# Two tokens per partition for the q and k transposes, reordered first loads, and a first FFN tile that begins on two units

## The chip, the cores and the metric

The kernel runs on one core of a Trainium2 chip. The metric is the device time of one execution in microseconds, lower is better. The numbers of the profile come from one profiled execution.

## The reference

Sliding-window causal attention (batch 8, 8 heads, 576 tokens, head size 64, window 64) feeds a gated FFN. All inputs and the output are float32.

```python
scores = scale * np.matmul(q, k.transpose(0, 1, 3, 2))
mask = (rel >= 0) & (rel < window)            # rel = query position - key position, window = 64
scores = np.where(mask, scores, -1000000000.0)
attn = np.exp(scores - max) / sum
attn_out = np.matmul(attn, v)                 # (8, 8, 576, 64)
x = attn_out.transpose(0, 2, 1, 3).reshape(4608, 512)
gate = np.maximum(x @ w_gate, 0.0)            # w_gate, w_val: 512 x 1536
val = x @ w_val
out = gate * val @ w_out                      # w_out: 1536 x 512, out: 4608 x 512
```

## The kernel before

**Attention units.** The 4608 tokens are cut into 24 units of 192 tokens, three per batch; a unit holds all eight heads. For each unit `u_load` brings q, k and v in, with four DMAs for q and four for k (two heads each, 32 partitions) and two for v. In q and k a partition holds six neighbouring tokens of a head, so 1536 bytes in a row. `u_cast` makes float16 copies on GpSimd (q of the first three units on ScalarE). `u_trans` transposes q and k in 32x32 blocks on VectorE, four instructions per unit, so that the head's elements lie on the partitions. Each writes with the step that the load's layout gives:

```python
nc.vector.transpose(dst.rearrange("p h (i j) -> p h j i", i=32),
                    src.rearrange("p (h j) e -> p h j e", h=2))
```

Here `i` runs over 32 partitions and `j` over the six tokens of each, so neighbouring results go six float16 elements (12 bytes) apart. `u_st` multiplies keys by queries on TensorE, `u_exp` takes the exponentials on ScalarE, `u_mask` zeroes on VectorE what lies outside the window, `u_pv` multiplies by v and sums the weights on TensorE, `u_copy` brings that to SBUF on ScalarE. `u_sum` (a transpose and a reciprocal), `u_back` (a transpose back) and `u_norm` (a product that writes the FFN's input `xt`) run on VectorE.

**FFN tiles.** `ffn(t)` works on one tile of tokens: 512 first, then ten of 384, and 256 last. For each of 12 slices of the hidden size it does two groups of four matmuls (`wg`, `wv`), a relu on ScalarE (`relu`) and a product on VectorE (`gate`, into `g_sb`). Then, for each 128 tokens, 12 matmuls with `wo` (`op`), a copy on ScalarE and a DMA out (`evac`). The hidden slices use four PSUM buffers (`f_ps`), attention four others (`a_ps`).

**The order.** All instructions are put in order when the program is built. `Weaver` keeps a planned clock that the FFN's matmuls (and a unit's scores and pv) advance, and a heap of pieces of attention work with planned times. Before each matmul group `advance` issues what is due. `plan_unit(u, T)` lays a unit's pieces around its time T: transposes from T - 6.8 (the first three units T - 2), scores at T, pv at T + 4.4, sums at T + 7.6, back at T + 8.9, norm at T + 9.9; loads at T - 22. Units 0 to 4 have times written by hand, later ones come every 13.2 planned us from 64. Ahead of a tile, `while normed[0] * U < starts[t] + sizes[t]: W.pop()` issues pieces early until all the tile's tokens are normed. Within an engine, instructions run in the order in which they were issued.

**The weights.** Nine chunks of 1 MB (three each of gate, value and out) go through three stage buffers (`w_load`); `w_cast` makes them float16, one half on GpSimd and one on ScalarE. All nine and the units' loads are issued on SyncE's queue (SP); only the q of unit 0 is issued on ScalarE's.

Of the kernel before, what the change touches and what calls it, by code (L numbers as in the profile page):

```python
# [9 lines left out]
FP32 = mybir.dt.float32  # L10
FP16 = mybir.dt.float16
# [31 lines left out]
def kernel(  # L43
# [19 lines left out]
    NF = DF // 128  # L63
    G = 4
    scale = 1.0 / float(D) ** 0.5
    sizes = [512] + [384] * 10 + [256]
    starts = [sum(sizes[:i]) for i in range(len(sizes))]
    assert sum(sizes) == NT

# [51 lines left out]
    def w_load(wt, src, j):  # L121
        stg = stage.tile([128, 4, 512], FP32, name="stg")
        if wt is wo:
            nc.sync.dma_start(stg, src.rearrange("(c p) n -> p c n", p=128)[:, 4 * j:4 * j + 4])
        else:
            nc.sync.dma_start(stg, src.rearrange("(c p) n -> p c n", p=128)[:, :, 512 * j:512 * j + 512])
        return stg

    def w_cast(wt, j, stg, half):
        cs = slice(2 * half, 2 * half + 2)  # L130
        dst = wo[:, 4 * j + 2 * half:4 * j + 2 * half + 2] if wt is wo else wt[:, cs, 512 * j:512 * j + 512]
        if half == 0:
            nc.gpsimd.tensor_copy(dst, stg[:, cs])
        else:
            nc.scalar.copy(dst, stg[:, cs])

    def u_load(u):
        b, uu = divmod(u, UB)  # L140
        d = units[u] = {}
        for name, src in (("k", k), ("q", q)):
            nat = d[name] = a_in.tile([128, 2, 384], FP32, name=name + "n")
            for g in range(G):
                eng = nc.scalar if (u == 0 and name == "q") else nc.sync
                eng.dma_start(
                    nat[32 * g:32 * g + 32],
                    src[b, 2 * g:2 * g + 2, U * uu:U * uu + U].rearrange(
                        "h (i j) d -> i h (j d)", i=32))
        vn = d["v"] = a_in.tile([128, 2, H, 64], FP32, name="vn")  # L150
        for w in range(2):
            k0 = U * uu - 64 + 128 * w
            p0 = max(0, -k0)
            nc.sync.dma_start(vn[p0:128, w], v[b, :, k0 + p0:k0 + 128].rearrange("h p d -> p h d"))

    def u_cast(u, name):
        d = units[u]
        if name == "v":
            v16 = d["v16"] = a_16.tile([128, 2, H, 64], FP16, name="v16")
            if u % UB == 0:  # L160
                nc.gpsimd.memset(v16[0:64, 0], 0.0)
                nc.gpsimd.tensor_copy(v16[64:128, 0], d["v"][64:128, 0])
                nc.gpsimd.tensor_copy(v16[:, 1], d["v"][:, 1])
            else:
                nc.gpsimd.tensor_copy(v16, d["v"])  # L165
        else:
            c16 = d[name + "16"] = a_16.tile([128, 768], FP16, name=name + "16")
            src = d[name].rearrange("p h e -> p (h e)")
            if name == "q" and u < UB:
                nc.scalar.copy(c16, src)  # L170
            else:
                nc.gpsimd.tensor_copy(c16, src)  # L172

    def u_trans(u, name, dh):
        d = units[u]
        src = d[name + "16"].rearrange("p (b e) -> p b e", e=64)[:, :, 32 * dh:32 * dh + 32]
        if name == "q":
            if dh == 0:
                d["qT"] = a_16.tile([128, 2, 2, U], FP16, name="qT")
            dst = d["qT"][:, dh]  # L180
        else:
            c0 = 64 + U * (u % UB)
            dst = kTs[(u // UB) % 2][:, dh, :, c0:c0 + U]
        nc.vector.transpose(dst.rearrange("p h (i j) -> p h j i", i=32),  # L184
                            src.rearrange("p (h j) e -> p h j e", h=2))

    def u_st(u):
        d = units[u]
# [23 lines left out]

    def u_mask(u, g):
        p = units[u]["p"][g]
        nc.vector.tensor_tensor(  # L215
            p, p, mask.rearrange("p w c -> p (w c)")[:, None, :].to_broadcast([128, 2, 256]), MUL)

    def u_pv(u):
# [46 lines left out]
        normed[0] = u + 1  # L265

    def plan_unit(u, T):
        fast = u < UB
        if not fast:
            W.at(T - 22, lambda: u_load(u))  # L270
        s = 0.5 if fast else 1.7
        for i, (name, dh) in enumerate((("k", 0), ("k", 1), ("q", 0), ("q", 1))):
            W.at(T - s * (4 - i), lambda name=name, dh=dh: u_trans(u, name, dh))
        for i, name in enumerate(("k", "q", "v")):
            W.at(T - s * 4 - (1.0 if fast else 4 - i), lambda name=name: u_cast(u, name))
        W.at(T, lambda: u_st(u))
        for g in range(G):
            W.at(T + 0.8 + 0.6 * g, lambda g=g: u_exp(u, g))
            W.at(T + 1.5 + 0.6 * g, lambda g=g: u_mask(u, g))
        W.at(T + 4.4, lambda: u_pv(u))  # L280
        for g in range(G):
            W.at(T + 5.2 + 0.5 * g, lambda g=g: u_copy(u, g))
        W.at(T + 7.6, lambda: u_sum(u))
        W.at(T + 8.9, lambda: u_back(u))
        W.at(T + 9.9, lambda: u_norm(u))


    def ffn(t):
        n = sizes[t]
        xt = xts[t]  # L290
        g_sb = g_sb_p.tile([128, NF, 512], FP16, name="g_sb")
        dt = 4 * n / 2400.0
        done = set()

        def relu(r_sb, h1):
            nc.scalar.activation(r_sb[:, 0:n], h1[:, 0:n], ACT.Relu)  # L296

        def gate(f, r_sb, h2):
            nc.vector.tensor_tensor(g_sb[:, f, 0:n], r_sb[:, 0:n], h2[:, 0:n], MUL)  # L299
            done.add(f)  # L300

        for f in range(NF):
            fs = bass.ds(f * 128, 128)
            hs = []
            for i, wt in enumerate((wg, wv)):
                W.advance(W.clock)
                h = f_ps.tile([128, 512], FP32, name=f"h{i}", tag="h")
                for c in range(NC):
                    nc.tensor.matmul(h[:, 0:n], wt[:, c, fs], xt[:, c, 0:n],  # L309
                                     start=(c == 0), stop=(c == NC - 1))  # L310
                hs.append(h)
                W.clock += dt
                if i == 0:
                    r_sb = f_sb.tile([128, 512], FP32, name="r_sb")
                    W.at(W.clock, lambda r_sb=r_sb, h=h: relu(r_sb, h))
                else:
                    W.at(W.clock, lambda f=f, r_sb=r_sb, h=h: gate(f, r_sb, h))

        def evac(sub, op):
            o_sb = f_sb.tile([128, DM], FP32, name="o_sb")  # L320
            nc.scalar.copy(o_sb, op)  # L321
            nc.sync.dma_start(out[bass.ds(starts[t] + sub * 128, 128)], o_sb)

        for sub in range(n // 128):
            op = f_ps.tile([128, DM], FP32, name="op", tag="h")
            ss = bass.ds(sub * 128, 128)
            for f0 in range(0, NF, 4):
                W.advance(W.clock)
                for f in range(f0, f0 + 4):
                    while f not in done:  # L330
                        W.pop()
                    nc.tensor.matmul(op, g_sb[:, f, ss], wo[:, f],  # L332
                                     start=(f == 0), stop=(f == NF - 1))
                W.clock += 4 * 512 / 2400.0
            W.at(W.clock, lambda sub=sub, op=op: evac(sub, op))

    with tc.manual_schedule():
        for u in range(UB):
            u_load(u)
        constants()  # L340
        at = 21.0
        for half in range(3):
            for wt, src in ((wg, moe_w_gate), (wv, moe_w_val)):
                def go(wt=wt, src=src, j=half, at=at):
                    stg = w_load(wt, src, j)
                    for hf in range(2):
                        W.at(at, lambda hf=hf: w_cast(wt, j, stg, hf))
                W.at(at - 12.0, go)
                at += 2.8
        for j in range(3):  # L350
            def go(j=j, at=at):
                stg = w_load(wo, moe_w_out, j)
                for hf in range(2):
                    W.at(at, lambda hf=hf: w_cast(wo, j, stg, hf))
            W.at(at - 12.0, go)
            at += 2.8
        for u, T in enumerate((10.0, 15.3, 20.6, 46.0, 52.0)):
            plan_unit(u, T)
        for u in range(5, NU):
            plan_unit(u, 64.0 + 13.2 * (u - 5))  # L360
        W.advance(27.0)
        for t in range(len(sizes)):
            while normed[0] * U < starts[t] + sizes[t]:
                W.pop()
            ffn(t)
        W.drain()

# [29 lines left out]
```

## Time and profile before

| | us |
|---|---|
| runs shown (three) | 416.14, 416.37, 418.63; median 416.37 |
| the profiled execution | 418.46 |
| its span, first to last instruction | 416.7 |
| TensorE busy / VectorE / ScalarE / GpSimd | 348.0 / 310.5 / 188.3 / 79.7 |
| mean granted TensorE clock | 0.97 |

In lines of the profile, L184 is line 184 of the kernel. A group's row names line, engine, operation, output and input, shape and count, then busy time in us and the mean of one in ns, then the idle time of the engine just before these instructions and what ended it. A timeline row begins with the start and the length in us. A wait's row reads: who waited for whom, us in total, times, the longest.

### The profile page before, as it was taken

The numbers are of one execution on the slowest core, as the hardware profiler recorded it, in microseconds if no ns is written. First come the engines' busy times: TensorE is split into PE (matmuls) and PEld (weight loads), VectorE is DVE, ScalarE is ACT, GpSimd is POOL, SyncE is SP. The second block draws the span as 40 slices with busy tenths as digits, with TensorE's granted clock in tenths as the row PEclk, the third lists the DMA queues.
The fourth block names the chain that finished last, engine by engine and source line by source line (L and its number), as shares of the span: only waits on it lengthen the run. The fifth ranks groups of instructions, "written<-read, shape, count | busy, mean of one in ns | idle before, by whom it ended". The sixth has DMA issues, their size and how long they took to land.

```text
span 416.7 us, 8098 instructions
## 1 busy us (share of the span) xinstructions
PE 348.0 (84%) x3120; PEld 193.6 (46%) x3120; DVE 310.5 (75%) x448; ACT 188.3 (45%) x385; POOL 79.7 (19%) x103
## 2 busy tenths in 40 slices
PE   0333696969798898798899799899899899799996
PEld 0222242435444545455555445445446546446583
DVE  3877556895958978968987978977987988786231
ACT  2355272725344445355446336346436545445241
POOL 3330343232111211121213101211203202000000
PEclk9999999887989999999999999999999999899999
DMA  8972998378005507306516307307417324020011
GB/s 183 238 271 87 298 282 220 89 229 213 2 25 161 131 30 201 89 26 182 123 51 183 86 35 195 89 27 198 105 52 197 71 94 111 0 77 2 25 53 50
DMA packets 71159, 49.82 MB, mean 120 GB/s; under 512 B 49616, under 2 KB 61904, under 8 KB 71120
## 3 DMA queue, kind: packets, MB, share of 16 engines
q1 hardware_dynamic: 70800, 48.91, 43.0%
q8 instruction: 24, 0.39, 0.4%
q10 hardware_dynamic: 320, 0.39, 0.4%
q14 instruction: 15, 0.12, 0.1%
HBM read 39.85 MB, written 9.44 MB: 118 GB/s over the span
## 4 chain that ended last, share of the span: by engine, by line
PE 50%; DVE 32%; ACT 6%; issue 5%; DMA 5%; SPq 1%; POOL 0%; DVEq 0%; ACTq 0%; POOLq 0%
PE h L309 31%; PE op L332 12%; DVE qT L184 10%; DVE kT L184 6%; DVE sT L244 4%; PE pv L226 4%; DVE rs L252 4%; PE st L199 4%; DVE g_sb L299 3%; DVE xt L261 3%; ACT xs L239 3%; DMA kn<-in_k_dram 3%; DMA stg<-in_moe_w_out_dram 2%; ACT p L211 1%; DVE rT L246 1%
## 5 line engine op out<-in xcount | busy, mean ns | idle before, releaser
L309 PE MATMUL h<-xt,wg 128*128 128x384 f16 (+2 forms) x576 | 123.2, 338 | 18.4 <-DVE xt L261 12.0
L309 PE MATMUL h<-xt,wv 128*128 128x384 f16 (+2 forms) x576 | 122.7, 337 | 1.2 <-DVE g_sb L299 1.2
L299 DVE TENSOR_TENSOR g_sb<-r_sb,h 128x384 f16<-128x384 f32 (+2 forms) x144 | 80.0, 562 | 57.3 <-PE h L309 42.8
L296 ACT ACTIVATE r_sb<-h 128x384 f32<-128x384 f32 (+2 forms) x144 | 71.1, 494 | 97.6 <-PE h L309 86.0
L332 PE MATMUL op<-wo,g_sb 128*128 128x512 f16 x432 | 99.9, 387 | 4.2 <-ACT r_sb L296 4.2
L309 PEld LDWEIGHTS <-wg 128*128 128x128 f16 x576 | 56.6, 100 | 61.7 <-issue 27.5
L309 PEld LDWEIGHTS <-wv 128*128 128x128 f16 x576 | 56.9, 101 | 41.8 <-issue 7.6
L184 DVE STREAM_TRANSPOSE kT<-k 128x384 f16<-128x384 f16 x48 | 69.0, 1456 | 6.1 <-POOL k L172 6.1
L211 ACT ACTIVATE p<-st 128x512 f16<-128x512 f32 x96 | 52.6, 608 | 38.5 <-PE st L199 38.0
L184 DVE STREAM_TRANSPOSE qT<-q 128x384 f16<-128x384 f16 x48 | 68.9, 1448 | 0.0
L332 PEld LDWEIGHTS <-g_sb 128*128 128x128 f16 x432 | 41.9, 100 | 54.9 <-ACT r_sb L296 4.7
L215 DVE TENSOR_TENSOR p<-p,mask 128x512 f16<-128x512 f16 x96 | 41.3, 451 | 20.5 <-ACT p L211 19.7
L321 ACT COPY o_sb<-op 128x512 f32<-128x512 f32 x36 | 21.1, 586 | 60.9 <-PE op L332 58.8
L199 PE MATMUL st<-qT,kT 32*128 32x128 f16 x768 | 20.0, 228 | 34.1 <-DVE qT L184 33.9
L239 ACT COPY xs<-pv 128x384 f32<-128x384 f32 x96 | 40.0, 498 | 14.3 <-PE pv L226 14.3
L172 POOL CAST k<-kn 128x768 f16<-128x768 f32 x24 | 20.7, 861 | 114.0 <-DMA kn<-in_k_dram 69.2
L199 PEld LDWEIGHTS <-kT 32*128 32x128 f16 x768 | 13.1, 97 | 44.0 <-issue 31.6
L244 DVE STREAM_TRANSPOSE sT<-xs 128x768 f32<-128x768 f32 x24 | 23.6, 982 | 12.1 <-ACT xs L239 12.1
L226 PE MATMUL pv<-p,v 128*64 128x128 f16 x384 | 25.7, 232 | 7.2 <-DVE p L215 7.2
L165 POOL CAST v<-vn 128x1024 f16<-128x1024 f32 x16 | 16.6, 1040 | 60.8 <-PE pv L226 35.7
L261 DVE TENSOR_TENSOR xt<-xs,rs 128x768 f16<-128x768 f32 (+2 forms) x35 | 26.9, 794 | 0.1
L172 POOL CAST q<-qn 128x768 f16<-128x768 f32 x21 | 17.4, 827 | 48.4 <-DVE qT L184 35.8
(27 smaller groups left out, 133.3 us busy)
## 6 DMA issues: line engine op xcount, KB each, us to landing
vn<-in_v_dram SPq DMA_DIRECT2D x40, 256.0 KB, 3.9
kn<-in_k_dram SPq DMA_DIRECT2D x96, 96.0 KB, 3.5
out_dram<-o_sb SPq DMA_DIRECT2D x36, 256.0 KB, 2.0
qn<-in_q_dram SPq DMA_DIRECT2D x92, 96.0 KB, 2.9
stg<-in_moe_w_gate_dram SPq DMA_DIRECT2D x3, 1024.0 KB, 6.7
stg<-in_moe_w_val_dram SPq DMA_DIRECT2D x3, 1024.0 KB, 7.2
stg<-in_moe_w_out_dram SPq DMA_DIRECT2D x3, 1024.0 KB, 7.3
vn<-in_v_dram SPq DMA_DIRECT2D x8, 128.0 KB, 2.9
```

Of the source, the lines that this page charges most:

```text
L184: nc.vector.transpose(dst.rearrange("p h (i j) -> p h j i", i=32), src.rearrange("p (h j) e -> p h j e", h=2))
L199: nc.tensor.matmul(d["st"][g][:, (2 * hh + w) * 128:(2 * hh + w + 1) * 128], kT[rows, dh, hh, ks + 128 * w:ks + 128 * w + 128], d["qT"][ro ...
L211: nc.scalar.activation(d["p"][g].rearrange("p h c -> p (h c)"), d["st"][g], ACT.Exp, scale=scale)
L215: nc.vector.tensor_tensor(p, p, mask.rearrange("p w c -> p (w c)")[:, None, :].to_broadcast([128, 2, 256]), MUL)
L226: nc.tensor.matmul(pv[64 * e:64 * e + 64, s, 64 * w:64 * w + 128], d["v16"][:, w, 2 * g + e] if s == 0 else (ones0 if u % UB == 0 and w == ...
L239: nc.scalar.copy(d["xs"][:, g], d["pv"][g])
L244: nc.vector.transpose(sT.rearrange("p g b c -> p g (b c)"), d["xs"][:, :, 1])
L261: nc.vector.tensor_tensor(xt_tile(t)[:, :, a - t0:z - t0], d["xs"][:, :, 0, a - lo:z - lo], rs[:, :, a - lo:z - lo], MUL)
L296: nc.scalar.activation(r_sb[:, 0:n], h1[:, 0:n], ACT.Relu)
L299: nc.vector.tensor_tensor(g_sb[:, f, 0:n], r_sb[:, 0:n], h2[:, 0:n], MUL)
L309: nc.tensor.matmul(h[:, 0:n], wt[:, c, fs], xt[:, c, 0:n], start=(c == 0), stop=(c == NC - 1))
L332: nc.tensor.matmul(op, g_sb[:, f, ss], wo[:, f], start=(f == 0), stop=(f == NF - 1))
```

## The change

- **Layout.** The 192 tokens of a unit are taken as three blocks of 64, and a partition holds two neighbouring tokens of each block. A load's runs are 512 bytes, and the transposes write in steps of two elements (4 bytes). Loads of q and k are now one DMA per head, 16 per unit instead of eight; units 1 and 2 share one set (`qk_load(1, 2)`).
- **First loads.** For the first three units the second head of each pair is issued on ScalarE's queue. The order is q,k of unit 0, its v, q,k of units 1 and 2, their v. A small exponential is issued between them.
- **Engines.** q of unit 0 is cast on VectorE, other q on GpSimd. Both halves of each weight chunk are cast on GpSimd. Three masks of units 0 and 1 run on GpSimd.
- **Order.** Tile sizes become 512, 256, then ten of 384. Tile 0 begins its first two hidden slices with the 384 tokens of units 0 and 1 and does the other 128 tokens once unit 2 is normed. Planned times of loads, casts and units change; units from 5 on start at max(T4 + 8, 69).

```diff
-    sizes = [512] + [384] * 10 + [256]
+    sizes = [512, 256] + [384] * 10
...
-        if half == 0:
-            nc.gpsimd.tensor_copy(dst, stg[:, cs])
-        else:
-            nc.scalar.copy(dst, stg[:, cs])
+        nc.gpsimd.tensor_copy(dst, stg[:, cs])
...
+    def qk_load(u, n):
+        b, uu = divmod(u, UB)
         for name, src in (("k", k), ("q", q)):
+            nat = a_in.tile([128, 2, 3 * n, 128], FP32, name=name + "n", tag=f"{name}n{n}", bufs=3 - n)
             for g in range(G):
+                for h in range(2):
+                    eng = nc.scalar if u < UB and h == 1 else nc.sync
+                    eng.dma_start(
+                        nat[32 * g:32 * g + 32, h],
+                        src[b, 2 * g + h, U * uu:U * uu + U * n].rearrange(
+                            "(m i j) d -> i m (j d)", i=32, j=2))
...
-            if name == "q" and u < UB:
-                nc.scalar.copy(c16, src)
+            if name == "q" and u == 0:
+                nc.vector.tensor_copy(c16, src)
...
-        nc.vector.transpose(dst.rearrange("p h (i j) -> p h j i", i=32),
-                            src.rearrange("p (h j) e -> p h j e", h=2))
+        nc.vector.transpose(dst.rearrange("p h (m i j) -> p h m j i", i=32, j=2), src)
...
-        nc.vector.tensor_tensor(
+        eng = nc.gpsimd if (u == 0 and g > 1) or (u == 1 and g > 2) else nc.vector
+        eng.tensor_tensor(
...
+        if u > 4:
+            W.at(T - 22, lambda: qk_load(u, 1))
+            W.at(T - 22, lambda: v_load(u))
         for i, (name, dh) in enumerate((("k", 0), ("k", 1), ("q", 0), ("q", 1))):
-            W.at(T - s * (4 - i), lambda name=name, dh=dh: u_trans(u, name, dh))
+            W.at(T - (0.5 if u < 5 else 1.7) * (4 - i), lambda name=name, dh=dh: u_trans(u, name, dh))
         for i, name in enumerate(("k", "q", "v")):
-            W.at(T - s * 4 - (1.0 if fast else 4 - i), lambda name=name: u_cast(u, name))
+            W.at(T - (3.0 if u < 5 else 11 - i), lambda name=name: u_cast(u, name))
...
+        early = {}
+        if t == 0:
+            while normed[0] < 2:
+                W.pop()
+            for f in range(2):
+                for i, wt in enumerate((wg, wv)):
+                    early[f, i] = f_ps.tile([128, 512], FP32, name=f"h{i}", tag="h")
+                    hidden(early[f, i], wt, f, 0, 2 * U)
+        ready(t)
...
+                if (f, i) in early:
+                    h = early[f, i]
+                    hidden(h, wt, f, 2 * U, n)
...
+        qk_load(0, 1)
+        warm = consts.tile([128, 2], FP32)
+        nc.vector.memset(warm, 0.0)
+        nc.scalar.activation(warm[:, 1:2], warm[:, 0:1], ACT.Exp)
+        v_load(0)
+        qk_load(1, 2)
+        v_load(1)
+        v_load(2)
         constants()
...
+        t_load, t_land = 8.0, 19.5
+        for c in chunks[:6]:
+            W.at(t_load, lambda c=c, at=t_land: chunk(*c, at))
+            t_load, t_land = t_load + 2.7, t_land + 2.7
+        W.at(t_load, lambda: qk_load(3, 1))
+        W.at(t_load, lambda: v_load(3))
+        t_load, t_land = t_load + 6.0, t_land + 6.0
+        T3 = t_land + 4.0
+        for c in chunks[6:]:
+            W.at(t_load, lambda c=c, at=t_land: chunk(*c, at))
+            t_load, t_land = t_load + 2.7, t_land + 2.7
+        W.at(t_load, lambda: qk_load(4, 1))
+        W.at(t_load, lambda: v_load(4))
+        T4 = t_land + 7.0
+        for u, T in enumerate((7.2, 14.0, 19.0, T3, T4)):
             plan_unit(u, T)
         for u in range(5, NU):
-            plan_unit(u, 64.0 + 13.2 * (u - 5))
-        W.advance(27.0)
+            plan_unit(u, max(T4 + 8.0, 69.0) + 13.2 * (u - 5))
+        W.advance(26.0)
```

Here `chunk` loads one weight chunk and plans its two casts at `at`, and `hidden` is one group of four matmuls over the columns that it is given.

More of the change, by code (lines that the diff above doesn't have):

```diff
@@ L131, in w_cast, with v_load @@
         dst = wo[:, 4 * j + 2 * half:4 * j + 2 * half + 2] if wt is wo else wt[:, cs, 512 * j:512 * j + 512]
-        if half == 0:
-            nc.gpsimd.tensor_copy(dst, stg[:, cs])
-        else:
-            nc.scalar.copy(dst, stg[:, cs])
-    def u_load(u):
+        nc.gpsimd.tensor_copy(dst, stg[:, cs])
+    def qk_load(u, n):
         b, uu = divmod(u, UB)
-        d = units[u] = {}
         for name, src in (("k", k), ("q", q)):
-            nat = d[name] = a_in.tile([128, 2, 384], FP32, name=name + "n")
+            nat = a_in.tile([128, 2, 3 * n, 128], FP32, name=name + "n", tag=f"{name}n{n}", bufs=3 - n)
             for g in range(G):
[L145 to L150, printed above, removed]
+                for h in range(2):
[4 more added lines that the diff above has]
+                            "(m i j) d -> i m (j d)", i=32, j=2))
+            for i in range(n):
+                units.setdefault(u + i, {})[name] = nat[:, :, 3 * i:3 * i + 3]
+    def v_load(u):
+        b, uu = divmod(u, UB)
+        d = units[u]
+        vn = d["v"] = a_in.tile([128, 2, H, 64], FP32, name="vn", bufs=2)
         for w in range(2):
@@ L166, in u_cast @@
         else:
-            c16 = d[name + "16"] = a_16.tile([128, 768], FP16, name=name + "16")
-            src = d[name].rearrange("p h e -> p (h e)")
-            if name == "q" and u < UB:
-                nc.scalar.copy(c16, src)
+            c16 = d[name + "16"] = a_16.tile([128, 2, 3, 128], FP16, name=name + "16")
+            src = d[name]
+            if name == "q" and u == 0:
+                nc.vector.tensor_copy(c16, src)
             else:
@@ L175, in u_trans @@
         d = units[u]
-        src = d[name + "16"].rearrange("p (b e) -> p b e", e=64)[:, :, 32 * dh:32 * dh + 32]
+        src = d[name + "16"].rearrange("p h m (j e) -> p h m j e", j=2)[:, :, :, :, 32 * dh:32 * dh + 32]
         if name == "q":
@@ L267, in plan_unit @@
     def plan_unit(u, T):
[L268 to L271, printed above, removed]
+        if u > 4:
+            W.at(T - 22, lambda: qk_load(u, 1))
+            W.at(T - 22, lambda: v_load(u))
         for i, (name, dh) in enumerate((("k", 0), ("k", 1), ("q", 0), ("q", 1))):
-            W.at(T - s * (4 - i), lambda name=name, dh=dh: u_trans(u, name, dh))
+            W.at(T - (0.5 if u < 5 else 1.7) * (4 - i), lambda name=name, dh=dh: u_trans(u, name, dh))
         for i, name in enumerate(("k", "q", "v")):
-            W.at(T - s * 4 - (1.0 if fast else 4 - i), lambda name=name: u_cast(u, name))
+            W.at(T - (3.0 if u < 5 else 11 - i), lambda name=name: u_cast(u, name))
         W.at(T, lambda: u_st(u))
@@ L285, in plan_unit, with ready @@
         W.at(T + 9.9, lambda: u_norm(u))
+    def ready(t):
+        while normed[0] * U < starts[t] + sizes[t]:
+            W.pop()
     def ffn(t):
         n = sizes[t]
-        xt = xts[t]
+        xt = xt_tile(t)
         g_sb = g_sb_p.tile([128, NF, 512], FP16, name="g_sb")
-        dt = 4 * n / 2400.0
         done = set()
@@ L300, in gate, with hidden @@
             done.add(f)
+        def hidden(h, wt, f, c0, c1):
+            for c in range(NC):
+                nc.tensor.matmul(h[:, c0:c1], wt[:, c, f * 128:f * 128 + 128], xt[:, c, c0:c1],
+                                 start=(c == 0), stop=(c == NC - 1))
+            W.clock += 4 * (c1 - c0) / 2400.0
+        early = {}
+        if t == 0:
+            while normed[0] < 2:
+                W.pop()
+            for f in range(2):
[3 more added lines that the diff above has]
+        ready(t)
         for f in range(NF):
-            fs = bass.ds(f * 128, 128)
-            hs = []
             for i, wt in enumerate((wg, wv)):
                 W.advance(W.clock)
[L307 to L312, printed above, removed]
+                if (f, i) in early:
+                    h = early[f, i]
+                    hidden(h, wt, f, 2 * U, n)
+                else:
+                    h = f_ps.tile([128, 512], FP32, name=f"h{i}", tag="h")
+                    hidden(h, wt, f, 0, n)
                 if i == 0:
@@ L337 @@
     with tc.manual_schedule():
-        for u in range(UB):
-            u_load(u)
-        constants()
[L341 to L356, printed above, removed]
@@ L357, with chunk @@
-        for u, T in enumerate((10.0, 15.3, 20.6, 46.0, 52.0)):
+        qk_load(0, 1)
[6 more added lines that the diff above has]
+        v_load(2)
+        constants()
+        chunks = [(wt, src, j) for j in range(3) for wt, src in ((wg, moe_w_gate), (wv, moe_w_val))]
+        chunks += [(wo, moe_w_out, j) for j in range(3)]
+        def chunk(wt, src, j, at):
+            stg = w_load(wt, src, j)
+            for hf in range(2):
+                W.at(at, lambda hf=hf: w_cast(wt, j, stg, hf))
@@ L358 @@
+        W.at(t_load, lambda: qk_load(4, 1))
+        W.at(t_load, lambda: v_load(4))
+        T4 = t_land + 7.0
+        for u, T in enumerate((7.2, 14.0, 19.0, T3, T4)):
             plan_unit(u, T)
         for u in range(5, NU):
-            plan_unit(u, 64.0 + 13.2 * (u - 5))
-        W.advance(27.0)
+            plan_unit(u, max(T4 + 8.0, 69.0) + 13.2 * (u - 5))
+        W.advance(26.0)
         for t in range(len(sizes)):
-            while normed[0] * U < starts[t] + sizes[t]:
-                W.pop()
```

## The prediction

> **What bounds the kernel now.** I read the page's busy times and chain first, then the costliest groups.
>
> ```profile
> span 416.7 us, 8098 instructions
> PE 348.0 (84%) x3120; PEld 193.6 (46%) x3120; DVE 310.5 (75%) x448; ACT 188.3 (45%) x385; POOL 79.7 (19%) x103
> PE 50%; DVE 32%; ACT 6%; issue 5%; DMA 5%; SPq 1%; POOL 0%; DVEq 0%; ACTq 0%; POOLq 0%
> ...
> L184 DVE STREAM_TRANSPOSE qT<-q 128x384 f16<-128x384 f16 x48 | 68.9, 1448 | 0.0
> L244 DVE STREAM_TRANSPOSE sT<-xs 128x768 f32<-128x768 f32 x24 | 23.6, 982 | 12.1 <-ACT xs L239 12.1
> ```
>
> TensorE carries half of the chain, VectorE a third. Of VectorE's 310.5 us, some 138 are the 48 transposes of q and the 48 of k at L184. One takes 1.45 us for 384 elements, while the transpose of the sums, which writes 4-byte elements side by side, does 768 in 0.98. So the q,k transposes are slow for their size, and their 12-byte steps in the output are the visible difference.
>
> How much of this TensorE feels is read tile by tile. The windows below run from the first FFN matmul of a tile to that of the next (columns: stretch, length, PE busy, clock, DMA share, GB/s).
>
> ```profile
> 45.04:92.50 47.46, 39.79 (x272) 0.95 0.77 212
> 92.50:127.70 35.20, 31.79 (x260) 0.87 0.34 90
> 158.50:190.30 31.80, 27.60 (x260) 1.00 0.40 104
> 190.30:219.40 29.10, 27.44 (x260) 1.00 0.47 119
> 340.90:372.70 31.80, 29.53 (x292) 0.95 0.24 67
> ```
>
> From 92.5 to 372.7 nine 384-token tiles take 280.2 us, 31.1 each. What they would take with nothing to wait for stands near the end, where VectorE has run dry of attention work, and at the first tile:
>
> ```profile
> 45.04 1.87 PE L309 MATMUL h<-xt,wg 128*128 128x512 f16 x4 [4.43 <-DVE xt L261]
> 46.70 1.91 PE L309 MATMUL h<-xt,wv 128*128 128x512 f16 x4
> ...
> 53.76 1.03 PE L309 MATMUL h<-xt,wv 128*128 128x512 f16 x4
> 54.62 1.03 PE L309 MATMUL h<-xt,wg 128*128 128x512 f16 x4
> ...
> 371.99 0.81 PE L199 MATMUL st<-qT,kT 32*128 32x128 f16 x32
> 372.74 0.82 PE L309 MATMUL h<-xt,wg 128*128 128x384 f16 x4
> ...
> 376.74 0.30 PE L226 MATMUL pv<-p,v 128*64 128x128 f16 x4
> ...
> 377.76 0.82 PE L309 MATMUL h<-xt,wg 128*128 128x384 f16 x4
> ...
> 389.47 7.93 PE L332 MATMUL op<-wo,g_sb 128*128 128x512 f16 x36
> 397.24 0.60 PE L309 MATMUL h<-xt,wg 128*128 128x256 f16 x4
> ```
>
> From start to start, the 18 groups of four h matmuls of 384 columns between 377.76 and 389.47 take 0.65 us each (0.43 for 256 columns by proportion), a group of 512 columns 0.86; 36 op matmuls 7.77; a unit's scores 0.75 and its pv 1.02. A 384-token tile is thus 24 x 0.65 + 7.77 = 23.4, the 512-token one 24 x 0.86 + 48 x 0.216 = 31.1, the 256-token one 24 x 0.43 + 24 x 0.216 = 15.6, a unit 1.77. Two units and a tile are 26.9 against the measured 31.1: **4.2 us lost per tile**, and before any of it 45 us of start. The first groups at 45 run at half pace (1.7 against 0.86) after a long idle of TensorE. The waits name the losses, first between 81 and 360 us, then 45 to 81:
>
> ```profile
> PE st L199 <- DVE qT L184: 11.1, 11, 2.3
> PE h L309 <- DVE g_sb L299: 7.6, 7, 1.2
> PE h L309 <- DVE xt L261: 7.5, 6, 3.5
> ...
> PE op L332 <- ACT r_sb L296: 4.2, 1, 4.2
> ```
>
> All of the steady ones end on VectorE.
>
> **The transposes.** Same count, same 384 elements, but the output step goes from 12 to 4 bytes. The row of before that has 4-byte steps is the sum transpose: 768 elements in 0.98 us. Ends: 0.49 (half of it) and 1.45 (no gain). I take 0.58, near the low end, since that row has the step that the change makes: 0.49 plus half of a fixed part of some 0.18 (an estimate; the reciprocal of 24 elements, 0.30 in a row below, bounds any fixed part). The change could also cost more if 2-byte writes into 4-byte words were slow; no row shows that. [...] VectorE's load then falls by 96 x 0.87 = 84 us; per tile by eight transposes, 7.0 us of 31.
>
> **The loads.** These rows give the packets and the rate of weight loads (2 KB packets):
>
> ```profile
> DMA packets 71159, 49.82 MB, mean 120 GB/s; under 512 B 49616, under 2 KB 61904, under 8 KB 71120
> q1 hardware_dynamic: 70800, 48.91, 43.0%
> 24.00:26.00 2.00, 0.94 (x15) 0.75 (x16) 1.54 (x3) 2.00 (x5) 0.48 (x1) 1.00 1.05 391
> ```
>
> q and k rows fall from 1536 to 512 B, so 512 packets per unit become 1536. Weights at 391 GB/s over 16 engines make 84 ns for 2 KB. The queue's whole packet time is 0.430 x 16 x 416.7 = 2867 us; 9216 packets of 2 KB take 774, leaving 2093 for 49616 packets of 256 B and 12288 of 1536 B. A straight line in size through these gives 25 ns for 256 B, 67 for 1536 B and 34 for 512 B (estimates). A unit's q,k go from 34.5 to 52 us of engine time, over 16 engines **+1.1 us**. Ends: priced like 256 B packets +0.3, like 1536 B ones +4.3. In steady state the queues stand at a share of 0.40 and this is hidden; at the start, three units make +3.3 us (0.9 to 13). Issues per unit go from 10 to 18; at some 0.45 us each (four in 1.80 below) that is 8 us of SP's 13.4 per unit, and loads stand 11 planned us ahead of their casts, so I cost it at nothing; without that lead it would be 3.6 us per unit. At the start 16 issues on ACT's queue take 7.4 us and end before the first exp.
>
> **The start.** Rows of the timeline that carry it:
>
> ```profile
> 0.81 1.80 SPq L146 DMA_DIRECT2D kn<-in_k_dram  x4
> ...
> 20.05 1.04 POOL L165 CAST v<-vn 128x1024 f16<-128x1024 f32 x1 [2.23 <-DMA vn<-in_v_dram]
> ...
> 23.44 1.04 POOL L133 CAST wg<-stg 128x1024 f16<-128x1024 f32 x1 [2.34 <-DMA stg<-in_moe_w_gate_dram]
> ...
> 26.14 1.04 POOL L133 CAST wv<-stg 128x1024 f16<-128x1024 f32 x1 [1.66 <-DMA stg<-in_moe_w_val_dram]
> ...
> 44.29 1.87 DVE L261 TENSOR_TENSOR xt<-xs,rs 128x512 f16<-128x512 f32 x2
> ```
>
> and three groups, for their mean durations:
>
> ```profile
> L211 ACT ACTIVATE p<-st 128x512 f16<-128x512 f32 x96 | 52.6, 608 | 38.5 <-PE st L199 38.0
> ...
> L215 DVE TENSOR_TENSOR p<-p,mask 128x512 f16<-128x512 f16 x96 | 41.3, 451 | 20.5 <-ACT p L211 19.7
> ...
> L163 POOL CAST v<-vn 128x512 f16<-128x512 f32 x8 | 5.3, 660 | 4.3 <-DMA vn<-in_v_dram 4.1
> ```
>
> Before, twelve transposes (17 us) and three units in turn hold the first h to 45. Now two units are enough, and what is late next is the data. Unit 0: VectorE's new q cast (no row; below POOL's 1.04 for a third more elements, above nothing) stands ahead of its k transposes and waits for q, so they gain less than they could; scores end near 11, and the data below come later whatever it costs in these bounds. Unit 2's v lands at 20.05 + 3.3 = 23.4; POOL casts it (1.04), and behind it in POOL's order stands unit 1's last mask. POOL's mask is in no row: from 0.7 (its 128x512 cast) to 1.3 (twice that, for two inputs); I take 0.7, its nearest row. That is 25.1. Then pv of that group 0.5, unit 2's scores 1.0 (both above their full pace, on a TensorE that has idled), four exps 2.4, a mask 0.45, unit 1's rs 1.06 and xt 0.8 (rows below), which VectorE has planned behind unit 2's masks: 31.3. Beside it wg lands at 26.7 and wv at 29.4, each with two POOL casts now (2.1): 31.5. **First h at 31.5** instead of 45.04. Ends: 28 to 41, nearly all from the packets.
>
> Weights: ACT's half of the casts goes to POOL, +1.04 us per chunk there, hidden as long as a chunk's load (2.6 us at 391 GB/s) is longer; ACT's late casts no longer hold back stage buffers. But wo's first chunk is cast on POOL ahead of unit 3's k, and it is loaded behind unit 3's q,k,v: I reckon it lands near 50, unit 3's scores near 55, TensorE there at 53.5. With the two later wo chunks I put 3 us there (0 to 8), where before lost 4.2.
>
> **The tiles.** A tile now ends on whole units: tile t needs units up to 2t+1, not two thirds of 2t+2, and units are planned from 69 instead of 64. By the planned clock, tile 2 starts 1.3 us before its last unit's norm is due, and that margin improves by 0.34 per tile. From the start of pv to the first h, TensorE then has 4.2 us of work. The chain beside it:
>
> ```profile
> 211.97 0.30 PE L226 MATMUL pv<-p,v 128*64 128x128 f16 x4
> 214.09 0.98 DVE L244 STREAM_TRANSPOSE sT<-xs 128x768 f32<-128x768 f32 x1 [1.39 <-ACT xs L239]
> 215.10 0.30 DVE L246 RECIPROCAL rT<-sT 128x24 f32<-128x24 f32 x1
> 216.46 1.06 DVE L252 STREAM_TRANSPOSE rs<-rT 128x768 f32<-128x768 f32 x1
> 218.58 1.12 DVE L261 TENSOR_TENSOR xt<-xs,rs 128x512 f16<-128x512 f32 x2
> ```
>
> 2.1 to the sums, then 1.0 + 0.3 + 1.06 + 0.8 (xt's share of 1.12 until the first h, and the wait between), and some 0.9 of two short transposes between: 6.2. So TensorE waits 2.0 at tile 2, 1.7, 1.3, 1.0, 0.6, 0.3 after: **7 us**. The waits for qT and g_sb I expect mostly gone; 0.5 us per tile, **5 us**, for what stays.
>
> **The sum** for the span: 31.5 start + 2.5 slow first groups (three at +0.84) + 31.1 + 3 + 15.6 + 234 (ten tiles) + 37.2 (21 units) + 7 + 5 + 3.9 (after the last matmul: 416.7 less 397.24 + 15.6) = **371**. The profiled execution took 418.46, 1.8 above its span, and the median of the runs was 2.1 below that; so 371 for a run as well.
>
> **The rivals.**
>
> *Half a gain*: the transposes come to about 1.0 us. Loss per tile falls by half only: 10 x 1.5 more, and 2 at the start: 388. Chance 0.08.
>
> *It doesn't do what it says*: step size isn't the cause, transposes stay at 1.45. Tiles keep losing 4.2 instead of 1.2 (+30) and eight of them lie in the start (+5): 406. For it: no row here has 2-byte elements at 4-byte steps. Against: the sum transposes. Chance 0.07.
>
> *Data late*: small loads cost more than my line, as dear as 1536 B packets. First h 9.6 later, unit 3 some 4 later: 385. For it: at the start the queues are full. [...] Against: eight 96 KB loads from two queues overlap in before. Chance 0.08.
>
> *Slower*: the boundary. If unit 2t+1's norm is later than I count (gates, masks and transposes ahead of it on VectorE) each of ten tiles stalls, and TensorE restarts at half pace, as at 92.5 where a 3.5 us wait is followed by a clock of 0.87. It costs 45 us, the whole gain, from 4.5 us more per boundary, stall and slow restart together; at 6 it gives 431. Against: VectorE is 7 us per tile lighter. Chance 0.03.
>
> **How the numbers follow.** Forecast 371, chance 0.74. Its own terms spread it over about 358 to 386: start 28 to 38, boundary 0 to 14, wo 0 to 8. The range takes in data late and half a gain: 356 to 394; outside lie no gain, slower and the tails. Within 1% (4 us), about what can be told from no change, lies only the far end of no gain: same 0.02, slower 0.03, faster 0.95.
>
> **What would show it.** L184 near 580 ns; VectorE busy near 230; first h near 31 and released by xt or by the weight casts; windows of 27 to 29 us per tile with waits on xt that shrink; q1's packets near 95,000 at a share near 0.5. It is wrong if L184 stays above 1 us, if vn of unit 2 lands after 30, or if each boundary shows an xt wait above 3 us.

## The result and the profile after

The changed kernel takes 385.7 us (median of four runs, 385.0 to 392.8) beside 416.5 for the kernel before on the same chip: a ratio of 0.924, 95% interval 0.918 to 0.930. One of the four runs was disturbed and is left out of the ratio. The profiled execution took 385.5 with a span of 383.8. The forecast was 371, the range 356 to 394.

The page's first lines, its chain and the transposes of q and k:

```profile
span 383.8 us, 8377 instructions
PE 337.5 (88%) x3136; PEld 191.9 (50%) x3136; DVE 237.4 (62%) x437; ACT 178.7 (47%) x374; POOL 97.7 (25%) x117
...
q1 hardware_dynamic: 95952, 48.13, 45.3%
...
PE 70%; DVE 15%; DMA 5%; ACT 4%; SPq 4%; issue 2%; POOL 0%; DVEq 0%; ACTq 0%; POOLq 0%
...
L187 DVE STREAM_TRANSPOSE kT<-k 128x384 f16<-128x384 f16 x48 | 27.6, 582 | 3.2 <-POOL k L175 3.2
...
L187 DVE STREAM_TRANSPOSE qT<-q 128x384 f16<-128x384 f16 x48 | 27.5, 582 | 0.0
```

A transpose fell from 1.45 to 0.58 us, VectorE by 73 us, and its share of the chain from 32% to 15%. SP's own queue has grown in the chain from 1% to 4%. Below are TensorE's waits (who for whom, total, times, longest) and the windows from tile to tile: tile 0 with the first groups of tile 1, the rest of tile 1, then tiles 2, 3, 5 and 9. Their columns are stretch, length, the busy times of PE, PEld, DVE, ACT and POOL, then clock, DMA share and GB/s:

```profile
PE st L201 <- DVE qT L187: 14.5, 9, 9.8
PE h L309 <- DVE xt L264: 12.3, 9, 2.8
PE pv L229 <- DVE p L218: 8.4, 8, 2.1
PE h L309 <- ACT o_sb L340: 5.8, 1, 5.8
```

```profile
35.42:79.62 44.20, 37.63 (x269) 18.44 (x269) 23.60 (x36) 14.72 (x28) 20.00 (x22) 0.97 0.68 197
79.62:102.13 22.51, 19.87 (x205) 13.88 (x204) 15.70 (x32) 11.22 (x27) 5.14 (x7) 0.90 0.47 123
102.13:132.42 30.29, 27.37 (x261) 15.38 (x260) 19.25 (x36) 14.51 (x31) 4.56 (x5) 0.99 0.35 95
132.42:162.66 30.24, 28.42 (x260) 15.75 (x260) 19.34 (x36) 14.70 (x31) 6.02 (x8) 0.96 0.39 107
...
191.48:219.16 27.68, 27.10 (x261) 15.34 (x260) 19.46 (x36) 14.75 (x31) 4.93 (x6) 1.00 0.45 120
...
302.62:329.72 27.10, 27.10 (x261) 15.43 (x261) 19.21 (x37) 14.23 (x31) 7.23 (x8) 1.00 0.54 145
```

Tile 9 takes 27.1, which is TensorE's own work (26.9 counted). Tiles 2 and 3 take 30, and tile 1 holds a wait of 5.8 us that did not exist before. Its rows, from the timelines of SP, ScalarE and TensorE:

```profile
62.14 0.58 ACT L340 COPY o_sb<-op 128x512 f32<-128x512 f32 x1 [0.95 <-PE op L351]
...
65.23 4.91 SPq L143 DMA_DIRECT2D kn<-in_k_dram  x8
70.24 3.68 SPq L143 DMA_DIRECT2D qn<-in_q_dram  x8
74.02 1.01 SPq L157 DMA_DIRECT2D vn<-in_v_dram  x2
75.13 4.80 SPq L341 DMA_DIRECT2D out_dram<-o_sb  x4
...
78.98 0.58 ACT L340 COPY o_sb<-op 128x512 f32<-128x512 f32 x1 [6.68 <-DMA out_dram<-o_sb]
...
79.62 1.01 PE L309 MATMUL h<-xt,wv 128*128 128x256 f16 x4 [5.76 <-ACT o_sb L340]
```

Read upwards: h has no PSUM buffer because the fourth output copy of tile 0 has not run; that copy has no o_sb buffer (there are three) because the outputs have not left; the first was copied by 62.7, but its DMA stands on SP behind the loads of two units until 75.13.

### The profile page after: what moved, and what is told of

Its sections match the earlier page's. It is cut to its first block, busy times and chain, and to the rows that moved or that the text cites. A ratio compares the mean times of both kernels' runs of the same rounds, so it can differ in the third digit from the quotient of the medians.

```text
span 383.8 us, 8377 instructions
## 1 busy us (share of the span) xinstructions
PE 337.5 (88%) x3136; PEld 191.9 (50%) x3136; DVE 237.4 (62%) x437; ACT 178.7 (47%) x374; POOL 97.7 (25%) x117
## 3 DMA queue, kind: packets, MB, share of 16 engines
q1 hardware_dynamic: 95952, 48.13, 45.3%
## 4 chain that ended last, share of the span: by engine, by line
PE 70%; DVE 15%; DMA 5%; ACT 4%; SPq 4%; issue 2%; POOL 0%; DVEq 0%; ACTq 0%; POOLq 0%
PE h L309 49%; PE op L351 14%; PE pv L229 4%; ACT xs L242 3%; PE st L201 3%; SPq L143 3%; DVE xt L264 3%; DVE sT L247 3%; DVE rs L255 2%; DVE qT L187 2%; DVE kT L187 2%; DMA kn<-in_k_dram 2%; DMA qn<-in_q_dram 1%; DVE p L218 1%; DMA vn<-in_v_dram 1%
## 5 line engine op out<-in xcount | busy, mean ns | idle before, releaser
L309 PE MATMUL h<-xt,wg 128*128 128x384 f16 (+3 forms) x584 | 120.0, 329 | 12.5 <-DVE xt L264 12.3
L309 PE MATMUL h<-xt,wv 128*128 128x384 f16 (+3 forms) x584 | 119.8, 329 | 5.8 <-ACT o_sb L340 5.8
L304 DVE TENSOR_TENSOR g_sb<-r_sb,h 128x384 f16<-128x384 f32 (+2 forms) x144 | 77.3, 543 | 71.9 <-PE h L309 63.8
L309 PEld LDWEIGHTS <-wg 128*128 128x128 f16 x584 | 56.6, 99 | 53.5 <-issue 17.1
L213 ACT ACTIVATE p<-st 128x512 f16<-128x512 f32 x96 | 51.7, 606 | 25.5 <-PE st L201 20.1
L218 DVE TENSOR_TENSOR p<-p,mask 128x512 f16<-128x512 f16 x93 | 45.2, 505 | 20.3 <-ACT p L213 18.8
L175 POOL CAST q<-qn 128x768 f16<-128x768 f32 x23 | 20.5, 890 | 61.8 <-DMA qn<-in_q_dram 34.5
L201 PE MATMUL st<-qT,kT 32*128 32x128 f16 x768 | 17.4, 226 | 14.7 <-DVE qT L187 14.5
L187 DVE STREAM_TRANSPOSE kT<-k 128x384 f16<-128x384 f16 x48 | 27.6, 582 | 3.2 <-POOL k L175 3.2
L229 PEld LDWEIGHTS <-v 128*64 128x64 f16 x384 | 18.1, 116 | 19.3 <-issue 18.4
L187 DVE STREAM_TRANSPOSE qT<-q 128x384 f16<-128x384 f16 x48 | 27.5, 582 | 0.0
L229 PE MATMUL pv<-p,ones 128*64 128x128 f16 x384 | 26.3, 235 | 0.0
```

The source lines that it names most:

```text
L187: nc.vector.transpose(dst.rearrange("p h (m i j) -> p h m j i", i=32, j=2), src)
L201: nc.tensor.matmul(d["st"][g][:, (2 * hh + w) * 128:(2 * hh + w + 1) * 128], kT[rows, dh, hh, ks + 128 * w:ks + 128 * w + 128], d["qT"][ro ...
L213: nc.scalar.activation(d["p"][g].rearrange("p h c -> p (h c)"), d["st"][g], ACT.Exp, scale=scale)
L218: eng.tensor_tensor(p, p, mask.rearrange("p w c -> p (w c)")[:, None, :].to_broadcast([128, 2, 256]), MUL)
L229: nc.tensor.matmul(pv[64 * e:64 * e + 64, s, 64 * w:64 * w + 128], d["v16"][:, w, 2 * g + e] if s == 0 else (ones0 if u % UB == 0 and w == ...
L309: nc.tensor.matmul(h[:, c0:c1], wt[:, c, f * 128:f * 128 + 128], xt[:, c, c0:c1], start=(c == 0), stop=(c == NC - 1))
```

## The experiments

Each kernel was timed beside the kernel before on one chip; ratios are to that kernel. Two kernels were timed once and have no interval.

**The layout alone.** The kernel before with the new rows, one load per head, and the new transposes.

```diff
-                        "h (i j) d -> i h (j d)", i=32))
+                            "(m i j) d -> i m (j d)", i=32, j=2))
...
-        nc.vector.transpose(dst.rearrange("p h (i j) -> p h j i", i=32), ...)
+        nc.vector.transpose(dst.rearrange("p h (m i j) -> p h m j i", i=32, j=2), src)
```

> The kernel before with the new q,k layout alone (512-byte runs, 4-byte steps, one load per head), all else as it was. Theory 1, that the shorter transposes are the gain: L184's line falls from 1.45 to 0.58 us, the first h comes 12 x 0.87 = 10 us earlier (near 35), the tiles lose 1.5 instead of 4.2 us each, in all near 382. Rival, that the order of the start and the first loads bring the gain and transposes off the chain are hidden: 400 or more.

386.7 us, ratio 0.926 (0.918 to 0.934): as fast as the whole change. The transposes and three rows of TensorE's timeline:

```profile
L185 DVE STREAM_TRANSPOSE kT<-k 128x384 f16<-128x384 f16 x48 | 27.7, 583 | 5.8 <-POOL k L173 5.8
```

```profile
44.54 1.86 PE L309 MATMUL h<-xt,wg 128*128 128x512 f16 x4 [5.01 <-DVE xt L261]
93.38 0.81 PE L309 MATMUL h<-xt,wg 128*128 128x384 f16 x4 [1.06 <-DVE xt L261]
120.73 0.81 PE L309 MATMUL h<-xt,wg 128*128 128x384 f16 x4 [0.25 <-DVE xt L261]
```

Half of theory 1 holds: the gain is the layout's. But it lies in the tiles, which take 27.3 from 93.4 to 120.7 instead of 31; the first h stays at 44.5 and did not come 10 us earlier.

**All but the layout.** The changed kernel with six tokens per partition again, in the loads and the transposes.

```diff
-                            "(m i j) d -> i m (j d)", i=32, j=2))
+                            "(m i j) d -> i m (j d)", i=32, j=6))
```

> The changed kernel with the old layout put back (six tokens per partition, 1536-byte runs, 12-byte steps), the number of loads, their queues and all orders as changed. Theory 1: L187 back at 1.45 us and 406 us, as the prediction's rival without a gain. Rival, that the step is not what slows a transpose: L187 stays near 0.58 and the time near 385. If 512-byte runs cost anything at the start, the v of unit 2 lands earlier here by up to 3 us.

446.0 us, ratio 1.068 (1.060 to 1.076): slower than before. The step theory holds (L187 back at 1.45) and the price was far too small. The v of unit 2 was cast at 21.3 here and at 21.7 in the changed kernel, so the 512-byte runs cost the start at most some tenths.

```profile
L187 DVE STREAM_TRANSPOSE kT<-k 128x384 f16<-128x384 f16 x48 | 68.7, 1455 | 3.2 <-POOL k L175 3.2
```

```profile
PE st L201 <- DVE qT L187: 43.3, 20, 11.1
PE h L309 <- DVE xt L264: 25.9, 10, 4.4
```

```profile
42.75 1.44 PE L309 MATMUL h<-xt,wg 128*128 128x384 f16 x4 [1.65 <-DVE xt L264]
...
115.35 1.44 PE L309 MATMUL h<-xt,wg 128*128 128x384 f16 x4 [4.08 <-DVE xt L264]
152.35 1.44 PE L309 MATMUL h<-xt,wg 128*128 128x384 f16 x4 [4.41 <-DVE xt L264]
```

With slow transposes the new plan waits over 4 us for xt at the start of tiles 2 and 3, and TensorE then runs at half pace for some 5 us (from 115.35 to 120.42 an h group starts every 1.28 us, behind that every 0.65): the first of these tiles takes 37.0 us. The waits for xt are not all: of the 43.3 us for qT, some 21 come after the first h, inside the tiles. So the reordering costs 7% by itself and nothing beside the layout. Something in it still cost time in the changed kernel; the next two runs look for it.

**Outputs on another queue.**

```diff
-            nc.sync.dma_start(out[bass.ds(starts[t] + sub * 128, 128)], o_sb)
+            nc.scalar.dma_start(out[bass.ds(starts[t] + sub * 128, 128)], o_sb)
```

> The changed kernel with the output DMAs issued from ScalarE's queue instead of SP's. Theory 2: the 5.8 us wait of tile 1's h on the copy of an output (o_sb) comes from SP, where the output DMAs stand behind 18 load issues per unit; it goes, and with it some 2 us of half pace behind it: 378. Rival, that the DMA engines are busy with loads and the outputs land late in any case: the wait stays and 385.

381.0 us, ratio 0.912 (0.904 to 0.920); the profiled execution 378.0. The wait on o_sb is gone from TensorE's list; the first output is issued at 63.3, right behind its copy, instead of 75.1. Theory 2 holds for the wait. The median gains 4.8 us and not the nearly 8 counted; the intervals of the two ratios overlap, so the size is loose.

**Later units planned earlier.**

```diff
-            plan_unit(u, max(T4 + 8.0, 69.0) + 13.2 * (u - 5))
+            plan_unit(u, max(T4 + 8.0, 66.0) + 13.2 * (u - 5))
```

> The changed kernel with units 5 and later planned 3 us earlier (from 66 instead of 69). Theory 3: the waits of the first h on xt at tiles 2 to 6 (2.5, 2.8, 1.8, 1.7 and some tenths) come from the plan and fall by up to 3 us each: 10 us less with the slow restart behind the longest, 376. Rival, that they come from VectorE's own load, or that an earlier plan only moves them to waits for qT: within 3 us of 385.

372.5 us, ratio 0.893 (0.884 to 0.901). The waits for xt shrink to one, and TensorE has no idle time to speak of from 105 to 340 us (window: length, PE busy):

```profile
PE h L309 <- ACT o_sb L340: 5.6, 1, 5.6
PE h L309 <- DVE xt L264: 1.2, 1, 1.2
```

```profile
105.00:340.00 235.00, 234.70 (x2269) 133.69 (x2268) 168.05 (x315) 126.61 (x271) 49.88 (x58) 1.00 0.43 115
```

Theory 3 holds, with 13 us instead of the 10 forecast: one constant of the plan took back what the faster start had brought.

**Both together.**

> The changed kernel with the output DMAs on ScalarE's queue and units 5 and later planned from 66, the two that helped. If the two gains are apart in time they add: 386 - 4.8 - 13.2 = 368. Rival, that they share the slow restart at 80 us or that earlier units collide with the outputs: 371 to 373, no better than the earlier units alone.

366.3 us, ratio 0.876 (0.869 to 0.883). They add. It beats each of the two alone; its one wait of the first h on xt is the start's, 1.4 us.

**Other steps.** Three tokens per partition, and one in another run (j=1):

```diff
-                            "(m i j) d -> i m (j d)", i=32, j=2))
+                            "(m i j) d -> i m (j d)", i=32, j=3))
```

> The changed kernel with three tokens per partition: 768-byte runs, transposes that write in steps of 6 bytes. It measures the step against the transposes' time. [...] Rival B, that steps off a 4-byte grid are the cost: near 1.45.

> The changed kernel with one token per partition: 256-byte runs, transposes that write side by side (steps of 2 bytes). It shows whether 4 bytes is already the floor. If the price is straight in the step (0.58 at 4, 0.80 at 6, 1.45 at 12), L187 takes 0.36 us; if one element per cycle is the floor, 0.58. The packets of q and k double in number and halve in size: near 387 if that is hidden as 512-byte ones were, 395 if the start waits for them.

The k transposes of the two runs, 6 bytes first, then 2:

```profile
L187 DVE STREAM_TRANSPOSE kT<-k 128x384 f16<-128x384 f16 x48 | 37.8, 798 | 3.0 <-POOL k L175 3.0
```

```profile
L187 DVE STREAM_TRANSPOSE kT<-k 128x384 f16<-128x384 f16 x48 | 26.1, 550 | 4.1 <-POOL k L175 4.1
```

Steps of 2, 4, 6 and 12 bytes take 0.55, 0.58, 0.80 and 1.45 us. From 4 bytes on the price is straight, 0.109 us per byte of step; at 4 bytes it is 0.03 above that of 2 bytes. So the time grows with the step: 6 bytes came at the 0.80 of a straight line between 4 and 12. Rival B of the first of the two runs (near 1.45) falls, and the straight line below 4 bytes (0.36) falls too. Timed once each, the two kernels took 392.4 and 390.9 us, against 420.3 and 420.1 for the kernel before; the second lies between its two forecasts.

**Masks on VectorE.**

```diff
-        eng = nc.gpsimd if (u == 0 and g > 1) or (u == 1 and g > 2) else nc.vector
+        eng = nc.vector
```

> The changed kernel with all masks on VectorE. Theory 4: GpSimd's masks (1.2 us each, and VectorE's own masks beside them at 1.2 instead of 0.45) hold up unit 1 in the start; without them the k cast of unit 1 is 2 us earlier and so is the first h (33 instead of 35.4): 383. Rival, that unit 2's pieces ahead of unit 1's set the first h: it stays within 0.5 us of 35.4 and 385.

384.8 us, ratio 0.918 (0.910 to 0.926); first h at 34.8. Theory 4 brings under a third of what it promised and no time that the intervals show.

**Unit 2 later.**

```diff
-        for u, T in enumerate((7.2, 14.0, 19.0, T3, T4)):
+        for u, T in enumerate((7.2, 14.0, 21.0, T3, T4)):
...
-        W.advance(26.0)
+        W.advance(24.0)
```

> The changed kernel with unit 2 planned at 21 instead of 19 and the tile begun at a planned 24 instead of 26, so that unit 1's last copies on ScalarE do not stand behind unit 2's exps, and unit 2's masks less ahead of unit 1's norm on VectorE. Theory 5: those two orders are why the first h came at 35.4 and not at 31.5; it comes near 31 and the time falls by 3 us, less what the early groups then wait for unit 2: 383. Rival, that unit 2 only moves the wait behind the early groups: the first h is earlier, the time 385.

394.6 us, ratio 0.942 (0.935 to 0.950), slower than the changed kernel.

```profile
33.66 1.44 PE L309 MATMUL h<-xt,wg 128*128 128x384 f16 x4 [6.25 <-DVE xt L264]
44.09 0.59 PE L309 MATMUL h<-xt,wg 128*128 128x128 f16 x4 [4.14 <-DVE xt L264]
...
102.32 0.81 PE L309 MATMUL h<-xt,wg 128*128 128x384 f16 x4 [3.16 <-DVE xt L264]
```

The first h is 1.8 us earlier, then unit 2 is missing for 4.1, and the later tiles wait longer because they begin 2 planned us sooner while units 5 and on stay at 69. That mixes the effects of two edits, so it says little on theory 5; the lengthened waits speak for theory 3 once more.

**Weight casts on two engines.**

```diff
-        nc.gpsimd.tensor_copy(dst, stg[:, cs])
+        if half == 0:
+            nc.gpsimd.tensor_copy(dst, stg[:, cs])
+        else:
+            nc.scalar.copy(dst, stg[:, cs])
```

> The changed kernel with the second half of each weight chunk cast on ScalarE again, as before the change. Theory 6: at the start VectorE's masks and norm (1.2 to 1.8 us where 0.45 and 0.8 were counted) are slowed by GpSimd's casts beside them; with half of these gone, the first h comes 1 us or more earlier than 35.4, 384. Rival, that ScalarE's exps and copies then stand behind the casts, as they did in the kernel before: the first h comes later and the time is 387 or more.

386.2 us, ratio 0.922 (0.916 to 0.927): no gain. Rows of GpSimd's casts and VectorE's masks ahead of the first h in the changed kernel, then the same masks with the casts split:

```profile
28.23 2.21 POOL L132 CAST wv<-stg 128x1024 f16<-128x1024 f32 x2 [1.33 <-DMA stg<-in_moe_w_val_dram]
...
29.99 0.73 DVE L218 TENSOR_TENSOR p<-p,mask 128x512 f16<-128x512 f16 x1 [0.44 <-ACT p L213]
...
30.88 2.24 POOL L132 CAST wg<-stg 128x1024 f16<-128x1024 f32 x2 [0.43 <-DMA stg<-in_moe_w_gate_dram]
...
31.87 1.53 DVE L218 TENSOR_TENSOR p<-p,mask 128x512 f16<-128x512 f16 x2
```

```profile
29.48 0.42 DVE L221 TENSOR_TENSOR p<-p,mask 128x512 f16<-128x512 f16 x1 [0.45 <-ACT p L216]
...
31.08 0.78 DVE L221 TENSOR_TENSOR p<-p,mask 128x512 f16<-128x512 f16 x2
```

The masks are at 0.4 each again and the first h comes at 33.8, 1.6 us earlier (with the start unchanged, three other runs had it at 35.2, 35.5 and 35.5, so some 0.3 of it may be chance). Theory 6 is right that the casts beside them lengthen the masks and wrong on the worth: the wo chunk and unit 3 are then waited for a little longer (0.9 and 1.1), and the o_sb wait remains.

**The layout with two load queues,** on the kernel before, with three buffers for q and k:

```diff
-                    eng = nc.scalar if (u == 0 and name == "q") else nc.sync
+                    eng = nc.scalar if u < UB and h == 1 else nc.sync
```

> The kernel before with the new layout and the loads of units 0 to 2 split over SP's and ScalarE's queues (one more buffer for q and k, so that no load waits), all else as before. Theory 7: the layout alone left the first h at 44.5 because SP issued the 60 loads of the start one after another, until 25.5 us; with half of them on the other queue it comes near 37 and the time falls to 379. Rival, that other orders of the start (three units ahead of the first tile, casts on ScalarE) hold it: first h at 42 or later, 385.

387.6 us, ratio 0.923 (0.916 to 0.929), first h at 44.0: the forecast of theory 7 falls. SP's issuing does end earlier (the first weight load is issued at 20.8 instead of 25.5), but the first h does not follow. The run is no clean test of the theory, though. ScalarE, which here issues 24 loads first, comes to its cast of unit 0's q 8 us later than with the layout alone (first row):

```profile
7.88 0.83 ACT L171 CAST q<-qn 128x768 f16<-128x768 f32 x1
```

```profile
15.91 0.83 ACT L171 CAST q<-qn 128x768 f16<-128x768 f32 x1
```

What else holds the first h at 44, with three units to finish and ScalarE's casts between them, was not separated.

**All four that looked good.**

> The two that helped (outputs on ScalarE's queue, units from 66) with the two that brought the first h forward (all masks on VectorE: by 0.7 us; weight casts split over GpSimd and ScalarE: by 1.6). If the earlier start is kept, first h near 33.2 and 364 us. Rival, that a start 2 us earlier is given back at unit 3 and the wo chunks, as in the run with split casts alone: 366, as the two without it.

366.7 us (seven runs), ratio 0.876 (0.871 to 0.881): the same as with two. In its profiled execution, the slowest of the seven, the first h came at 35.3, so not even the earlier start was there. The loads were late in it: the first weight load was issued at 18.6, against 17.1 and 16.7 in the two runs that brought the first h forward. Why they were late is open.

## Why the prediction was right, and where it was mis-sized

The cause was right: the shorter transposes are the gain. The size was not: 45 us were forecast and 31 measured. The time stands at the upper end of what the forecast's own terms allowed (358 to 386), and its largest miss, the stop in tile 1, was in none of them, so that it still lies there is partly luck.

**The transposes** were as counted: 0.58, VectorE at 237 us (some 230 forecast). The single steps show why: going from 12 to 4 bytes takes 0.87 us off, going on to 2 bytes 0.03 more.

**The loads**: the +3.3 us at the start did not appear. q1's 95,952 packets at 45.3% of 383.8 us and 16 engines are 2782 us, and ScalarE's queue adds 80: 2862, with three times the packets for q and k, against 2867 and 27 before. So 512-byte packets cost no more in sum than a third as many of 1536 bytes; the straight line in size was wrong, and even the lower end of the bounds (0.3 us a unit) was not reached. With it the data-late rival falls: a 48 KB load of k or q landed in a median 2.2 or 1.9 us, a 96 KB one before in 3.5 or 2.9.

**First h** came at 35.4, not 31.5, although the data was there: unit 2's v was cast at 21.7, nearly two us ahead of my count. One missing term is an order on VectorE that the count left out: unit 0's norm ran between unit 2's transposes, so unit 2's scores began at 27.0 where the count has 25.6.

```profile
24.72 1.27 DVE L264 TENSOR_TENSOR xt<-xs,rs 128x768 f16<-128x768 f32 x1
...
27.03 0.30 PE L201 MATMUL st<-qT,kT 32*128 32x128 f16 x4 [1.62 <-DVE qT L187]
```

The other is VectorE beside GpSimd: a mask was counted at 0.45 and took up to 1.25 beside a cast, and GpSimd's own mask took 1.2 to 1.3, the upper end and not the 0.7 that I chose. With the casts split the first h came 1.6 of these 3.9 us earlier, with all masks on VectorE 0.7; the parts are not fully separated.

**Issues on SP "at nothing"** is the step that failed. I counted 8 us of SP's 13.4 per unit (the two units from 65.2 to 75.0 and from 80.0 to 90.3 took about 10), asked whether the loads come in time, and never who is queued behind them: the outputs. The trace put 5.8 us there and 2.1 more at half pace, in one place; taking the outputs off that queue removed the wait and gave 4.8 in the median, and 6.3 with the later units moved forward as well (366.3 against 372.5).

**Tile 0 and wo** lost 0.8 at waits instead of the 3 counted.

**The boundary** had the right cause. At tile 2 the chain from the start of pv to the first h took 6.3 (95.8 to 102.1) where 6.2 was counted; TensorE's work beside it was 3.8 instead of 4.2. Waits for xt of 2.5, 2.8, 1.8 and 1.7 were measured where 2.0, 1.7, 1.3 and 1.0 were forecast, then tenths. Tiles 2 to 10 took 254.6 us against 242.5 of plain work: 12 lost where 9.5 were counted. Moving the units forward was worth 13 in all.

Together against the 371: +3.9 first h, -2 tile 0, +9 tile 1 (29.7 us where 18.4 is plain work and 2.5 more was counted), +2.6 tiles 2 to 10 and -0.7 in the last tile are the 13 us by which the span of 383.8 exceeds it.

**The rivals.** "Doesn't do what it says" was priced 406 by letting each tile lose 4.2 us as before. The run without the layout gave 446: with slow transposes the boundary waits of the other rival, given 0.03, come on top (24 us for xt after the first h), and waits for qT with them. The two rivals were tied together, and I had priced them apart.

## What to carry to other kernels

Price a queue by what stands behind it, not only by whether its own work is in time: an output DMA behind some twenty load issues stopped TensorE through two buffers that nobody had on the list. A planned order is tuned to the durations it was planned with; after a large change of one duration, move the plan's constant before judging the rest of the change. And try the parts apart in both directions: here one part alone gave all of the gain, and the others alone were a loss. What the others are worth once the outputs' queue and the plan are mended is not known: no run gives the layout alone these two edits.

## What the runs showed of the hardware that was not expected

- A VectorE mask (two float16 inputs, 128x512) takes 0.42 us alone (69 of the changed kernel: 0.41 to 0.43) and up to 1.25 beside GpSimd's casts; the four transposes of q and k from 24.2 to 27.4, beside two casts, stay at 0.55 to 0.60. The longer masks end with GpSimd's instruction: in the changed kernel's rows, shown at the run with the split casts, GpSimd's casts end at 30.44 and 33.12 and the masks beside them at 30.72 and 33.40. All 19 masks of the changed kernel that began while GpSimd was at work on a cast or a mask ended 0.27 to 0.33 us after that one did.
- Half pace after a wait does not follow the length of the wait alone: in the changed kernel a wait of 2.5 us was followed by full pace and one of 2.8 by half,

```profile
102.13 0.81 PE L309 MATMUL h<-xt,wg 128*128 128x384 f16 x4 [2.53 <-DVE xt L264]
132.42 1.44 PE L309 MATMUL h<-xt,wg 128*128 128x384 f16 x4 [2.79 <-DVE xt L264]
```

but with the outputs on ScalarE's queue one of 3.3 was followed by full pace:

```profile
126.35 0.81 PE L309 MATMUL h<-xt,wg 128*128 128x384 f16 x4 [3.29 <-DVE xt L264]
```

So the length of the gap alone does not decide; what else does, no run here shows.
